# Four more idle matmuls on zeros between the second scores and the M1 of batch 0

**Chip, cores, metric.** One Trainium2 chip, one core. The metric is device time in microseconds (us) of one execution. Timed runs are compared with runs of the kernel before on the same chip in the same job. Ratios are the mean time of one kernel's fast runs over that of the other's fast runs of the same rounds, so they are not quite the ratio of the medians that are quoted beside them.

## The reference, cut to what matters

```python
p_packed = sm_attn(p, k, v)                  # 8 batches, 8 heads: 32 packed rows attend to 576 keys
x        = sm_attn(q, p_packed, p_packed)    # 576 queries attend to the 32 packed rows
h = x_as_tokens @ w_in                       # 4608 x 512 @ 512 x 2048
g = s * relu(h)**2 + b
out = g @ w_out                              # 2048 x 512
```

## The kernel before

The kernel is a fixed order of small steps ("words"). The words of batch 0 that matter here:

- `a` first attention (packed), which ends in `ppc` on VectorE; `c.0.0`, `c.0.1` second scores, the two halves of the columns, each followed by two exponentials on ScalarE;
- `w.0.0`, `w.0.1` the softmax's denominators: two matmuls, then `ld` (Ln) and `rcd` (Exp) on ScalarE, then `aT` on VectorE;
- `f.0.0`, `e.0.1`, `e.0.2`, `e.0.3` the four chunks of `pw` (packed rows times w_in), evicted by VectorE (f) or by ScalarE and VectorE (e); each needs its piece of w_in;
- `h.0.x` half groups of M1 (4 matmuls of 288 columns), evicted by `rlu` on ScalarE and squared on VectorE;
- `t`, the output matmuls `yps`; `z`, one idle matmul on zeros that is meant to keep TensorE's clock up.

```python
def big(dt=F32):                       # every TensorE result goes to such a tile: 2 x 512 float32 per partition
    w = NB if dt == F32 else 2 * NB
    rings["n"] += 1
    ps = rings["h"][rings["n"] % len(rings["h"])]      # two pools of 2 tiles: 4 tiles at this stage
    return ps.tile([P, 2, w], dt, tag="h", name="hps")

def idle(n):
    t = big()                          # an idle matmul takes a tile as well
    for x in range(n):
        mm(t[:, 0, :], zeros[:, 0:P], zeros[:], start=True, stop=True)

def weights_half(b, hf):               # the word w
    ...
    dps = big()
    for qd in range(NQ):
        mm(dps[:, qd, 0:HS], onesbd[:], e2[b][:, qd, cols], start=True, stop=True)
    ...
    act.activation(out=ld[:], in_=dps[:, :, 0:HS], func=AF.Ln)
    ...
    act.activation(out=rcd[:], in_=ld[:]..., func=AF.Exp, scale=-1.0)
    vec.tensor_tensor(out=aT[b][:, :, cols], in0=e2[b][:, :, cols], in1=rcd[:]..., op=ALU.mult)
```

The program pins the order of each engine's instructions (`keep_in_program_order`), and the trace of before has it: on ScalarE `ld` at 17.97, `rcd` at 18.67, the second pair at 19.26 and 19.93, then `pw` at 20.52 us. Which tile a word gets is decided when the program is built, and with it what it must wait for.

The softmax here doesn't subtract the row's maximum and nothing guards it: scores larger than these inputs give would overflow.

Of the kernel before, what the change touches and what calls it, by code (L numbers as in the profile page):

```python
# [13 lines left out]

ORDER = """
z kf kc kh.0.1 mask p.0.1 qh.0.0 qh.0.1 kT.0.1 kT.0.0 z z v.0 z win.0 win.1 pp2.0.1 pT.0 qT.0.1 z
s.0.0 s.0.1 qT.0.0 win.2 a.0.0 a.0.1 c.0.0 f.0.0 win.3 c.0.1 w.0.0 w.0.1 e.0.1 z h.0.2 h.0.0 e.0.2
wout.0 q.1 h.0.4 h.0.7 h.0.5 e.0.3 h.0.6 h.0.8 wout.1 h.0.1 h.0.11 h.0.13 k.1 h.0.3 four h.0.10 t.1
p.1.2 h.0.9 wout.2 t.2 h.0.15 qT.1.1 t.1 t.2 qT.1.0 b.0 t.0 h.0.12 t.0 v.1 b.1 pp2.1.2 t.1 kT.1.1
t.2 pT.1 wout.3 sb b.2 h.0.14 q.2 kT.1.0 t.1 t.0 t.0 b.3 s.1.0 s.1.1 t.0 t.1 k.2 t.1 p.2.8 a.1.0 b.4  # L20
a.1.1 q.3 b.5 b.6 b.7 c.1 t.1 t.0 t.1 e.1.0 w.1.0 t.0 t.0 w.1.1 v.3 t.2 qT.2.1 t.2 e.1.1 k.3 t.2 t.2
t.2 kT.2.0 pp2.2.8 m.1.0 three t.3 t.3 pT.2 kT.2.1 f.1.2 t.3 e.1.3 v.2 t.3 qT.2.0 t.3 m.1.8 m.1.1
m.1.6 m.1.14 m.1.13 m.1.3 t.3 m.1.5 m.1.10 qo.3 m.1.2 t.4 qD.3 s.2.0 m.1.7 m.1.9 m.1.11 t.4 s.2.1
m.1.4 m.1.12 kD.3 t.3 m.1.15 a.2.0 t.4 a.2.1 t.4 t.4 t.4 pT.3 k.4 c.2 t.4 t.4 t.3 E.2.0 w.2.0 t.6
t.6 t.5 w.2.1 t.6 t.5 t.5 vo.3 t.6 E.2.1 t.6 m.2.5 t.5 t.5 t.6 pT.4 t.6 s.3.0 s.3.1 t.6 m.2.1 t.5
m.2.3 a.3.0 m.2.13 t.5 m.2.10 a.3.1 t.7 q.4 t.7 t.7 c.3 t.5 qo.4 m.2.2 t.7 t.7 w.3.0 t.8 t.8 E.3.0
qD.4 t.8 t.8 kD.4 w.3.1 v.4 t.7 m.2.14 t.7 m.2.0 m.2.15 m.2.6 m.2.7 m.2.9 t.8 t.8 m.2.12 m.2.8
m.2.11 t.7 m.2.4 E.3.1 t.8 t.8 vo.4
"""

@with_exitstack
# [809 lines left out]
```

## Time and profile before

| | before |
|---|---|
| time, median of 3 (lowest to highest) | 255.1 us (254.94 to 255.21) |
| span of the profiled run | 252.8 us |
| busy: TensorE, VectorE, ScalarE | 95%, 57%, 57% |
| mean granted TensorE clock | 0.993 |
| first `yps` matmul of the output | 28.75 us |
| from there to the end | 224.1 us |

The mean clock is worth reading exactly: one window of 3.41 us at half clock (18.81 to 22.22 in the trace of before) lowers the mean over 252.8 us by 3.41 x 0.5 / 252.8 = 0.0067, so 0.993 is one halved window, about 0.987 two, 0.980 three (a halved piece at the very end takes up to 0.003 more: 1.3 us in the trace of before_again). The clock's first record begins at 11.98 us in the trace of before, and this is meant below where the clock "rose" at the start. Ahead of it matmuls of 512 columns start 0.43 us apart (9.43 to 9.86 in before), twice the 0.216 of the later ones at full clock.

The profiled execution of before took 254.62 us, 0.3 us less than the fastest of its timed runs: the trace that the prediction reads is of a quick execution.

The views that decide are shown in the prediction. One more, the order of time of TensorE before (start, length, engine, line, operation, count, idle before and its releaser):

```profile
16.98 1.46 PE L93 MATMUL hps<-e,onesbd 128*128 128x288 bf16 x4 [0.29 <-ACT e L104]
18.85 1.30 PE L93 MATMUL hps<-w_in_sb,ppc 64*32 64x512 bf16 x8 [0.42 <-DMA w_in_sb<-in_moe_w_in_dram]
20.48 2.00 PE L93 MATMUL hps<-aT,pw 128*128 128x288 bf16 x8
```

The first line is `w`: four matmuls that stream for 0.12 us each (288 columns; M1's of this width start 0.122 us apart at full clock), spread over 1.46 us because each waits for one exponential. "Busy" in the windows counts each matmul's modelled length (0.28 us for one of these) and overstates how much streams.

### The profile page before, as it was taken

The numbers are of one execution on the slowest core, as the hardware profiler recorded it, in microseconds if no ns is written. First come the engines' busy times: TensorE is split into PE (matmuls) and PEld (weight loads), VectorE is DVE, ScalarE is ACT, GpSimd is POOL, SyncE is SP. The second block draws the span as 40 slices with busy tenths as digits, with TensorE's granted clock in tenths as the row PEclk, the third lists the DMA queues.
The fourth block names the chain that finished last, engine by engine and source line by source line (L and its number), as shares of the span: only waits on it lengthen the run. The fifth ranks groups of instructions, "written<-read, shape, count | busy, mean of one in ns | idle before, by whom it ended". The sixth has DMA issues, their size and how long they took to land.

```text
span 252.8 us, 5625 instructions
## 1 busy us (share of the span) xinstructions
PE 240.3 (95%) x2326; PEld 137.5 (54%) x2326; DVE 145.3 (57%) x301; ACT 143.4 (57%) x220; POOL 32.8 (13%) x49
## 2 busy tenths in 40 slices
PE   0869999999999999999999999999999999999994
PEld 0644655457745656655565556645665545555442
DVE  3347742597657578666835676467734664453221
ACT  3178923738856698668664774478545854543000
POOL 8736242110021002100110021000000000000000
PEclk9997999999999999999999999999999999999999
DMA  7999999999679985996699679909412122111332
GB/s 147 190 201 205 204 203 205 195 239 212 117 124 185 183 148 89 220 181 137 134 174 194 124 148 163 225 22 178 99 38 52 34 60 70 41 41 44 83 83 83
DMA packets 54635, 34.61 MB, mean 137 GB/s; under 512 B 27345, under 2 KB 50129, under 8 KB 54609
## 3 DMA queue, kind: packets, MB, share of 16 engines
q0 software_dynamic: 24928, 18.32, 48.7%
q1 hardware_dynamic: 29584, 15.87, 27.5%
q8 instruction: 18, 0.29, 0.5%
q14 instruction: 9, 0.07, 0.1%
q10 hardware_dynamic: 96, 0.07, 0.1%
HBM read 37.23 MB, written 9.44 MB: 185 GB/s over the span
## 4 chain that ended last, share of the span: by engine, by line
PE 89%; DMA 4%; POOL 3%; ACT 1%; DVE 1%; issue 1%; POOLq 0%
PE yps L93 52%; PE hps L93 35%; DMA w_in_sb<-in_moe_w_in_dram 4%; PE hps L96 2%; POOL raw L104 2%; ACT rlu L104 1%; POOL w_in_sb L104 1%; DVE ysb L104 0%; ACT pw L104 0%; DVE pw L104 0%; POOL pn L104 0%; POOL identb L104 0%; POOLq L104 0%; POOLq L825 0%
## 5 line engine op out<-in xcount | busy, mean ns | idle before, releaser
L93 PE MATMUL yps<-w_out_sb,gT 128*128 128x512 bf16 (+2 forms) x592 | 144.6, 374 | 0.2 <-DVE ysb L104 0.2
L104 ACT ACTIVATE rlu<-hps 128x576 bf16<-128x576 f32 x128 | 80.6, 653 | 58.9 <-PE hps L93 52.9
L104 DVE TENSOR_TENSOR gT<-rlu 128x576 bf16<-128x576 bf16 x128 | 58.2, 456 | 57.6 <-ACT rlu L104 55.5
L93 PE MATMUL hps<-aT,pw 128*128 128x288 bf16 x512 | 80.7, 288 | 0.2 <-DVE pw L104 0.2
L93 PEld LDWEIGHTS <-gT 128*128 128x128 bf16 x592 | 53.5, 98 | 49.7 <-issue 7.2
L93 PEld LDWEIGHTS <-pw 128*128 128x128 bf16 x512 | 50.0, 99 | 31.8 <-issue 1.2
L104 DVE SCALAR_TENSOR_TENSOR ysb<-yps,svec,biasrep 128x512 f32<-128x512 f32 (+2 forms) x37 | 27.0, 732 | 16.5 <-PE yps L93 16.4
L104 DVE TENSOR_SCALAR pw<-hps,rd 128x1024 bf16<-128x1024 f32 (+1 forms) x22 | 22.5, 1036 | 1.0 <-PE hps L93 0.4
L104 ACT ACTIVATE pw<-hps,rd 128x1024 bf16<-128x1024 f32 (+1 forms) x18 | 17.5, 973 | 3.8 <-PE hps L93 3.7
L104 DVE TENSOR_TENSOR aT<-e,rcd 128x576 bf16<-128x576 bf16 x16 | 12.1, 757 | 9.9 <-ACT rcd L104 9.8
L104 POOL DMA_DIRECT2D raw<-in_k_dram x8 | 6.2, 779 | 85.2 <-DMA kT<-raw 62.5
L104 ACT ACTIVATE e<-hps,rs 128x576 bf16<-128x576 f32 (+1 forms) x18 | 11.3, 686 | 10.1 <-PE hps L93 10.1
L104 ACT ACTIVATE e<-hps 96x768 bf16<-96x768 f32 x16 | 12.5, 800 | 3.6 <-PE hps L93 3.5
L96 PE MATMUL hps<-identb,raw 96*64 96x96 bf16 (+1 forms) x216 | 9.5, 224 | 5.3 <-DMA raw<-in_k_dram 5.2
L96 PEld LDWEIGHTS <-raw 96*64 96x64 bf16 (+1 forms) x216 | 8.1, 117 | 8.2 <-DMA raw<-in_k_dram 6.0
L93 PE MATMUL hps<-w_in_sb,ppc 64*32 64x512 bf16 x256 | 11.6, 389 | 0.7 <-DMA w_in_sb<-in_moe_w_in_dram 0.4
L104 ACT ACTIVATE rcd<-ld 128x576 f32<-128x576 f32 x16 | 10.9, 683 | 0.5
L104 ACT ACTIVATE ld<-hps 128x576 f32<-128x576 f32 x16 | 10.3, 644 | 0.3 <-PE hps L93 0.2
L104 DVE COPY raw<-raw 96x1536 bf16<-96x1536 bf16 x20 | 10.4, 562 | 0.0
L93 PEld LDWEIGHTS <-ppc 64*32 64x32 bf16 x384 | 4.0, 89 | 9.4 <-issue 6.9
L93 PEld LDWEIGHTS <-raw 96*64 96x64 bf16 (+1 forms) x264 | 7.7, 106 | 2.5 <-issue 1.5
L104 POOL DMA_DIRECT2D raw<-in_q_dram x11 | 8.4, 777 | 3.8 <-PE hps L96 3.3
(45 smaller groups left out, 105.6 us busy)
## 6 DMA issues: line engine op xcount, KB each, us to landing
raw<-in_v_dram POOLq DMA_DIRECT2D x8, 576.0 KB, 11.2
out_dram<-ysb SPq DMA_DIRECT2D x23, 192.0 KB, 2.5
raw<-in_q_dram POOLq DMA_DIRECT2D x7, 576.0 KB, 11.8
raw<-in_k_dram POOLq DMA_DIRECT2D x7, 576.0 KB, 8.1
out_dram<-ysb SPq DMA_DIRECT2D x24, 128.0 KB, 2.4
w_in_sb<-in_moe_w_in_dram POOLq DMA_DIRECT2D x8, 256.0 KB, 10.8
w_out_sb<-in_moe_w_out_dram POOLq DMA_DIRECT2D x4, 512.0 KB, 14.8
out_dram<-ysb SPq DMA_DIRECT2D x23, 64.0 KB, 2.1
```

Source lines behind the costliest of these rows:

```text
L93: return tc.keep_in_program_order(nc.tensor.matmul(*a, **kw))
L96: return tc.keep_in_program_order(nc.tensor.transpose(*a, **kw))
L104: return lambda *a, **kw: tc.keep_in_program_order(f(*a, **kw))
```

## The change

Its intent: fill TensorE's waits between batch 0's second scores and its M1 with work on zeros, so that the clock isn't halved there.

```diff
-s.0.0 s.0.1 qT.0.0 win.2 a.0.0 a.0.1 c.0.0 f.0.0 win.3 c.0.1 w.0.0 w.0.1 e.0.1 z h.0.2 h.0.0 e.0.2
+s.0.0 s.0.1 qT.0.0 win.2 a.0.0 a.0.1 c.0.0 f.0.0 z win.3 c.0.1 z w.0.0 z w.0.1 e.0.1 z z h.0.2 h.0.0
+e.0.2 ...   (the rest of the order is the same, wrapped anew)
```

More of the change, by code (lines that the diff above doesn't have):

```diff
@@ L16 @@
 z kf kc kh.0.1 mask p.0.1 qh.0.0 qh.0.1 kT.0.1 kT.0.0 z z v.0 z win.0 win.1 pp2.0.1 pT.0 qT.0.1 z
-s.0.0 s.0.1 qT.0.0 win.2 a.0.0 a.0.1 c.0.0 f.0.0 win.3 c.0.1 w.0.0 w.0.1 e.0.1 z h.0.2 h.0.0 e.0.2
-wout.0 q.1 h.0.4 h.0.7 h.0.5 e.0.3 h.0.6 h.0.8 wout.1 h.0.1 h.0.11 h.0.13 k.1 h.0.3 four h.0.10 t.1
-p.1.2 h.0.9 wout.2 t.2 h.0.15 qT.1.1 t.1 t.2 qT.1.0 b.0 t.0 h.0.12 t.0 v.1 b.1 pp2.1.2 t.1 kT.1.1
-t.2 pT.1 wout.3 sb b.2 h.0.14 q.2 kT.1.0 t.1 t.0 t.0 b.3 s.1.0 s.1.1 t.0 t.1 k.2 t.1 p.2.8 a.1.0 b.4
-a.1.1 q.3 b.5 b.6 b.7 c.1 t.1 t.0 t.1 e.1.0 w.1.0 t.0 t.0 w.1.1 v.3 t.2 qT.2.1 t.2 e.1.1 k.3 t.2 t.2
-t.2 kT.2.0 pp2.2.8 m.1.0 three t.3 t.3 pT.2 kT.2.1 f.1.2 t.3 e.1.3 v.2 t.3 qT.2.0 t.3 m.1.8 m.1.1
-m.1.6 m.1.14 m.1.13 m.1.3 t.3 m.1.5 m.1.10 qo.3 m.1.2 t.4 qD.3 s.2.0 m.1.7 m.1.9 m.1.11 t.4 s.2.1
-m.1.4 m.1.12 kD.3 t.3 m.1.15 a.2.0 t.4 a.2.1 t.4 t.4 t.4 pT.3 k.4 c.2 t.4 t.4 t.3 E.2.0 w.2.0 t.6
-t.6 t.5 w.2.1 t.6 t.5 t.5 vo.3 t.6 E.2.1 t.6 m.2.5 t.5 t.5 t.6 pT.4 t.6 s.3.0 s.3.1 t.6 m.2.1 t.5
-m.2.3 a.3.0 m.2.13 t.5 m.2.10 a.3.1 t.7 q.4 t.7 t.7 c.3 t.5 qo.4 m.2.2 t.7 t.7 w.3.0 t.8 t.8 E.3.0
-qD.4 t.8 t.8 kD.4 w.3.1 v.4 t.7 m.2.14 t.7 m.2.0 m.2.15 m.2.6 m.2.7 m.2.9 t.8 t.8 m.2.12 m.2.8
-m.2.11 t.7 m.2.4 E.3.1 t.8 t.8 vo.4
+s.0.0 s.0.1 qT.0.0 win.2 a.0.0 a.0.1 c.0.0 f.0.0 z win.3 c.0.1 z w.0.0 z w.0.1 e.0.1 z z h.0.2 h.0.0
+e.0.2 wout.0 q.1 h.0.4 h.0.7 h.0.5 e.0.3 h.0.6 h.0.8 wout.1 h.0.1 h.0.11 h.0.13 k.1 h.0.3 four
+h.0.10 t.1 p.1.2 h.0.9 wout.2 t.2 h.0.15 qT.1.1 t.1 t.2 qT.1.0 b.0 t.0 h.0.12 t.0 v.1 b.1 pp2.1.2
+t.1 kT.1.1 t.2 pT.1 wout.3 sb b.2 h.0.14 q.2 kT.1.0 t.1 t.0 t.0 b.3 s.1.0 s.1.1 t.0 t.1 k.2 t.1
+p.2.8 a.1.0 b.4 a.1.1 q.3 b.5 b.6 b.7 c.1 t.1 t.0 t.1 e.1.0 w.1.0 t.0 t.0 w.1.1 v.3 t.2 qT.2.1 t.2
+e.1.1 k.3 t.2 t.2 t.2 kT.2.0 pp2.2.8 m.1.0 three t.3 t.3 pT.2 kT.2.1 f.1.2 t.3 e.1.3 v.2 t.3 qT.2.0
+t.3 m.1.8 m.1.1 m.1.6 m.1.14 m.1.13 m.1.3 t.3 m.1.5 m.1.10 qo.3 m.1.2 t.4 qD.3 s.2.0 m.1.7 m.1.9
+m.1.11 t.4 s.2.1 m.1.4 m.1.12 kD.3 t.3 m.1.15 a.2.0 t.4 a.2.1 t.4 t.4 t.4 pT.3 k.4 c.2 t.4 t.4 t.3
+E.2.0 w.2.0 t.6 t.6 t.5 w.2.1 t.6 t.5 t.5 vo.3 t.6 E.2.1 t.6 m.2.5 t.5 t.5 t.6 pT.4 t.6 s.3.0 s.3.1
+t.6 m.2.1 t.5 m.2.3 a.3.0 m.2.13 t.5 m.2.10 a.3.1 t.7 q.4 t.7 t.7 c.3 t.5 qo.4 m.2.2 t.7 t.7 w.3.0
+t.8 t.8 E.3.0 qD.4 t.8 t.8 kD.4 w.3.1 v.4 t.7 m.2.14 t.7 m.2.0 m.2.15 m.2.6 m.2.7 m.2.9 t.8 t.8
+m.2.12 m.2.8 m.2.11 t.7 m.2.4 E.3.1 t.8 t.8 vo.4
 """
```

## The prediction

Its sums come to 0.13 us faster (step 3), 0.21 us slower (step 4) and 255.1 us at even chances. In the paragraph that begins with "one window of 3.41 us", "them" are the instructions of ScalarE and VectorE, and the four tiles are the program's two pools of two. The 0.43 us of an idle matmul at half clock is twice 0.216, as M1's 0.240 is twice 0.122; it is also the spacing of the idle matmuls ahead of the clock's first record.

> **What bounds the kernel now.** I read the page first. Its second part cuts the span of 252.8 us into 40 slices of 6.3 us; these are the rows of TensorE, ScalarE and the granted TensorE clock, in tenths:
>
> ```profile
> PE   0869999999999999999999999999999999999994
> ACT  3178923738856698668664774478545854543000
> PEclk9997999999999999999999999999999999999999
> ```
>
> TensorE is full from slice 4 (19 us) on, so the kernel is TensorE-bound for nine tenths of its length and any time saved or lost before that shifts everything behind it. The one mark on the clock is the 7 in slice 4. So I cut the stretch around it into pieces of 3.41 us (columns: window, length, then busy us and count of TensorE, weight loads, VectorE, ScalarE, GpSimd; granted clock; DMA share; GB/s):
>
> ```profile
> 11.98:15.40 3.42, 2.93 (x105) 2.61 (x104) 0.92 (x2) 2.54 (x4) 0.94 (x2) 1.00 1.21 194
> 15.40:18.81 3.41, 2.04 (x36) 0.80 (x34) 1.94 (x5) 2.36 (x6) 1.21 (x2) 1.00 1.24 206
> 18.81:22.22 3.41, 3.27 (x17) 1.43 (x17) 2.18 (x3) 2.88 (x5) 2.25 (x3) 0.50 1.23 204
> 22.22:25.64 3.42, 3.23 (x36) 1.99 (x35) 2.69 (x6) 3.24 (x7) 2.31 (x3) 1.00 1.25 206
> ```
>
> The clock is halved for exactly one such window, 18.81 to 22.22, and the window before it is the one with the least TensorE work (2.04 us busy, against 2.93 and more). That is the target of the change: batch 0's softmax (c, w), where TensorE waits for ScalarE.
>
> Then the chain of work that ended last, for 14 to 36 us (start, length, what):
>
> ```profile
> 8.55 10.93 DMA w_in_sb<-in_moe_w_in_dram
> 19.53 2.97 PE hps L93 x16
> 22.52 0.65 ACT rlu L104
> ...
> 25.23 0.73 ACT pw L104
> 25.96 0.02 issue
> 25.98 0.76 DVE pw L104
> 26.75 0.04 issue
> 26.79 2.12 PE hps L93 x16
> ```
>
> Until 19.5 us the path is the load of w_in. Then come 3 us of TensorE at half clock; but from 22.5 to 26.8 the path is ScalarE and VectorE, not TensorE. That decides how much a faster TensorE is worth. The order of time on ScalarE there (start, length, what, count, idle before and its releaser):
>
> ```profile
> 16.42 1.68 ACT L104 ACTIVATE e<-hps,rs 128x288 bf16<-128x288 f32 x4 [1.77 <-PE hps L93]
> 17.97 0.67 ACT L104 ACTIVATE ld<-hps 128x576 f32<-128x576 f32 x1
> 20.52 0.67 ACT L104 ACTIVATE pw<-hps,rd 128x512 bf16<-128x512 f32 x1
> 21.69 0.65 ACT L104 ACTIVATE rlu<-hps 128x576 bf16<-128x576 f32 x1 [0.50 <-PE hps L93]
> 22.52 0.65 ACT L104 ACTIVATE rlu<-hps 128x576 bf16<-128x576 f32 x1 [0.18 <-PE hps L93]
> ```
>
> ScalarE is busy without a pause from 16.42 to 21.19, waits 0.50 and 0.18 us for the two slow M1 groups (h.0.2, h.0.0), and hardly pauses again before 28 us. Those 0.68 us are all that a warm clock can give back to ScalarE.
>
> [...]one window of 3.41 us at 0.50, and its M1 matmuls (288 columns) start 0.240 us apart, against 0.122 us at full clock. [...]the trace has them in program order everywhere I looked, so a late ld delays all that follows it on ScalarE. [...]there are four tiles at this stage, and every idle matmul takes one: it isn't free even where TensorE waits.
>
> **The change, part by part.** The built programs show what it does: ScalarE, VectorE, GpSimd and SyncE have exactly the same instructions and waits; TensorE gets four weight loads and four 128x512 matmuls; and because each takes a PSUM tile, eleven or so waits in this stretch change. From the first M1 groups after the fourth chunk of pw onwards everything is the same again.
>
> 1. The four matmuls themselves. A 512-column one costs 0.216 us of TensorE at full clock (the spacing of the later yps matmuls: 28.746 to 28.962), 0.43 at half. One comes before c.0.1 (16.38 to 16.60): c.0.1 then ends at 16.91 instead of 16.69, but ScalarE takes it only at 17.21; free. One before w.0.0, one between w.0.0 and w.0.1: TensorE waits there anyway. The fourth is behind e.0.1, which waits for w_in until 19.49; it ends near 20.2 (warm) and h.0.2 can't start before aT is ready; free when warm.
>
> 2. A new wait, the cost of the change. w.0.0 used to start with one exponential done each (matmuls at 16.98 and 17.37), so ScalarE ran ld directly behind the four exponentials, at 17.97. Now the extra tiles push w.0.0 onto the tile that c.0.1 has just used, so it waits for the fourth exponential, which ends at 18.10. Then 0.05 us of semaphore (17.317 to 17.368 in the trace), 0.12 to the second matmul, 0.28 its length, 0.04 to ScalarE: ld starts at 18.59, 0.62 us later. ScalarE's queue moves with it: both ld/rcd pairs, aT (VectorE 20.01 instead of 19.39), pw of e.0.1 (ScalarE 21.13, VectorE ends 22.68 instead of 22.06).
>
> 3. The gain, if the clock stays full. h.0.2 waits for aT, so it starts at about 20.88 (before 20.48), and needs 0.49 instead of 0.96 us: ends 21.53. ScalarE's rlu then follows pw without a pause at 21.70 (before 21.69), the next at 22.23 (22.52): of the 0.68 us of pauses, 0.62 were spent on the late ld. e.0.2 no longer waits for an rlu, but its w_in lands at 22.01, so it starts at 22.05; h.0.4 needs VectorE's pw: 22.73 (22.76 before). pw of e.0.2 on ScalarE 22.76 (23.07), rlu of h.0.4 at 23.42 (23.64): 0.2 us ahead. Then e.0.3: its last piece of w_in lands at 24.61 in the trace, and it started at 24.59 and 24.65 before. It can't move, so its pw starts at 25.10 at best instead of 25.23. Sum: 0.13 us faster.
>
> 4. If the clock still drops. e.0.1 at 19.53, two idle matmuls of 0.43, h.0.2 at 20.94, its rlu at 22.15 (before 21.69), h.0.0's at 22.75 (22.52), pw of e.0.3 at 25.44 (25.23). Sum: 0.21 us slower.
>
> Which of the two? Columns streamed in the window from 15.40: about 1.1 us before (0.15 of packed, 0.12 + 0.12 of c, 0.22 of f, 4 x 0.12 of w), 32%; now plus 3 x 0.216, 51%. The window ahead of it, by the same rough count about 2.2 us or 65%, did not drop the clock. 51% lies in the middle of the bracket; I call it even.
>
> **Rivals.** (a) The full prize of the throttle: 3.41 us at half clock is 1.7 us of lost array time, so 253.4 us. For it speaks that TensorE bounds the rest; against it the chain, which from 22.5 to 26.8 runs over ScalarE and VectorE, and w_in's landings at 22.01 and 24.61. (b) The late ld goes through undiminished, 0.62 us: 255.7 us. That needs ScalarE's pauses of 0.68 us not to close; only if the clock drops and the window falls otherwise. (c) The matmuls cost their own time on the path: 4 x 0.216 = 0.86 us, 256.0 us. Against it: each stands in a wait. (d) [...]other executions drop the clock elsewhere than this profile. The three timed runs lie within 0.27 us of each other, so this is small.
>
> **Range and chances.** Even chances of -0.13 and +0.21 give 255.1 us. Run-to-run spread (254.94 to 255.21) and an error of some tenths in the waits make the range 254.5 to 255.7. Two per cent is 5.1 us, three times the whole loss to the clock; I give 0.98 to "within 2%", 0.01 to each side.
>
> **What would show it.** ld of batch 0 near 18.6 instead of 17.97, and aT near 20.0: step 2. The granted clock in the window from about 18.8: 1.00 is step 3, 0.50 step 4; h.0.2's matmuls 0.122 or 0.240 apart. ScalarE's pause before the first rlu gone: step 3. The e.0.3 matmuls still near 24.6 and the first M1 group after pw of e.0.3 at 26.6 to 27.0 instead of 26.79: the sum. From there to the end the same length, 226.1 us. I am wrong if that group moves by over half a microsecond, or if the rest of the span changes length.

## The result

The changed kernel took 254.6 us (median of 4 runs, 254.37 to 254.96) against 255.12 us (4 runs, 254.94 to 255.21): ratio 0.9982, 95% interval 0.9964 to 0.9999. The profiled run was the slowest of its four, at a mean clock of 1.000. It is inside the predicted range. But the two traces do not show where half a microsecond went, and the profiled span, 253.2 us, is longer than before's 252.8.

The page's rows of TensorE and the granted clock after, 40 slices of the span in tenths:

```profile
PE   0877999999999999999999999999999999999994
PEclk9999999999999999999999999999999999999999
```

The 7 of the clock is gone. The windows of 3.41 us, on this run's own boundaries (window, length, busy us and count of TensorE, weight loads, VectorE, ScalarE, GpSimd; granted clock; DMA share; GB/s):

```profile
12.31:15.72 3.41, 2.67 (x104) 2.41 (x102) 0.92 (x2) 2.25 (x4) 0.63 (x2) 1.00 1.20 192
15.72:19.14 3.42, 2.40 (x40) 1.12 (x36) 1.95 (x5) 1.79 (x4) 2.29 (x3) 1.00 1.24 205
19.14:22.55 3.41, 2.50 (x29) 1.13 (x27) 1.51 (x3) 3.34 (x6) 1.96 (x3) 1.00 1.24 205
```

The stretch that was at 0.50 is at 1.00. TensorE in order of time after; the third line is `w.0.0`, which now waits for the fourth exponential:

```profile
17.05 0.39 PE L93 MATMUL hps<-zeros 128*128 128x512 bf16 x1
17.37 0.32 PE L93 MATMUL hps<-qT,ppc 64*32 64x288 bf16 x8
18.70 0.40 PE L93 MATMUL hps<-e,onesbd 128*128 128x288 bf16 x2 [0.59 <-ACT e L104]
```

ScalarE in order of time after:

```profile
16.79 1.86 ACT L104 ACTIVATE e<-hps,rs 128x288 bf16<-128x288 f32 x4 [1.96 <-PE hps L93]
19.15 0.65 ACT L104 ACTIVATE ld<-hps 128x576 f32<-128x576 f32 x1 [0.49 <-PE hps L93]
21.67 0.67 ACT L104 ACTIVATE pw<-hps,rd 128x512 bf16<-128x512 f32 x1
22.24 1.18 ACT L104 ACTIVATE rlu<-hps 128x576 bf16<-128x576 f32 x2
25.57 0.70 ACT L104 ACTIVATE pw<-hps,rd 128x512 bf16<-128x512 f32 x1
```

The two `rlu` now follow `pw` without the pauses of 0.50 and 0.18 us, and a new pause of 0.49 us stands before `ld`: from the first exponential to `ld` it is 2.36 us, against 1.55 before. The end of this stretch in the chain of work (start, length, what):

```profile
25.57 0.71 ACT pw L104
26.30 0.76 DVE pw L104
27.11 2.12 PE hps L93 x16
```

The same three links as before, 0.32 us later. Ahead of them the chain has changed: before, it was the load of w_in until 19.49, then TensorE at half clock; now it is ScalarE's queue, from the late `ld` at 19.15 to this `pw` with no wait for another engine. All of the 0.32 us was there before the changed stretch: the load of `v.0` landed at 14.46 us in this trace and at 14.08 in the one before, and `ppc` on VectorE, which starts batch 0's second attention, was at 16.06 instead of 15.69. Counted from `ppc`, the first `yps` matmul comes after 13.00 us (before: 13.06), and 224.1 us remain in both. In these two traces the change is worth 0.06 us after `ppc`: the late `ld` took what the clock gave. So the half microsecond between the medians had to come from executions that were not profiled.

### The profile page after: what moved, and what is told of

Same layout as the page of the kernel before. It is cut to its first block, busy times and chain, and to the rows that moved or that the text cites. A ratio compares the mean times of both kernels' runs of the same rounds, so it can differ in the third digit from the quotient of the medians.

```text
span 253.2 us, 5632 instructions
## 1 busy us (share of the span) xinstructions
PE 239.6 (95%) x2330; PEld 137.3 (54%) x2330; DVE 145.1 (57%) x301; ACT 143.5 (57%) x220; POOL 32.8 (13%) x49
## 4 chain that ended last, share of the span: by engine, by line
PE 89%; DMA 3%; ACT 3%; POOL 2%; DVE 1%; issue 1%; POOLq 0%; ACTq 0%
PE yps L93 52%; PE hps L93 35%; DMA raw<-in_v_dram 3%; PE hps L96 2%; POOL raw L104 1%; ACT rlu L104 1%; ACT pw L104 1%; ACT rcd L104 1%; ACT ld L104 0%; DVE ysb L104 0%; ACT e L104 0%; DVE pw L104 0%; POOL pn L104 0%; POOL identb L104 0%; DVE ppc L104 0%
## 5 line engine op out<-in xcount | busy, mean ns | idle before, releaser
L93 PE MATMUL hps<-aT,pw 128*128 128x288 bf16 x512 | 79.8, 286 | 1.6 <-DVE aT L104 0.9
L104 DVE TENSOR_TENSOR aT<-e,rcd 128x576 bf16<-128x576 bf16 x16 | 12.1, 758 | 10.5 <-ACT rcd L104 10.4
L104 ACT ACTIVATE e<-hps,rs 128x576 bf16<-128x576 f32 (+1 forms) x18 | 11.4, 685 | 10.4 <-PE hps L93 10.3
L93 PE MATMUL hps<-w_in_sb,ppc 64*32 64x512 bf16 x256 | 11.0, 382 | 0.0
L104 DVE COPY raw<-raw 96x1536 bf16<-96x1536 bf16 x20 | 10.4, 561 | 0.0
L93 PE MATMUL hps<-e,raw 96*64 96x32 bf16 (+1 forms) x264 | 8.5, 188 | 0.7 <-DMA raw<-in_v_dram 0.7
```

Source lines behind the costliest of these rows:

```text
L93: return tc.keep_in_program_order(nc.tensor.matmul(*a, **kw))
L104: return lambda *a, **kw: tc.keep_in_program_order(f(*a, **kw))
```

## The experiments

Theory: the new waits make `ld` late by about 0.6 us, the full clock closes ScalarE's pauses, and the time depends on which windows are halved. Rivals: the clock alone gives TensorE its lost time back; the tiles' new places are the gain; the loads of `v.0` and w_in make all differences. Each kernel gave a correct result. After each label: median, median of before in the same job, ratio with its 95% interval.

**before_again**: no edit.

> The kernel before against itself, to show how far two medians of five rounds lie apart when nothing differs. All theories: ratio 1.000, medians within 0.2 us; clock 0.993 in nearly all runs (one halved window of 3.41 us at about 19 us). If some of its runs show 1.000, the phase of the window decides and not the kernel alone.

254.93 us against 255.15 us; 0.9989 (0.9965 to 1.0012). Nothing differs, and the result is 0.1% with an interval of 0.5%. The clocks were 0.993 in 2 of 6 runs and 0.984 to 0.987 in 4: two halved windows are the common case, and the trace of before had shown the rarer one. The trace of this run has two (columns as above):

```profile
16.35:19.76 3.41, 3.25 (x37) 0.91 (x38) 1.76 (x5) 2.70 (x6) 1.96 (x3) 0.50 1.24 206
19.76:23.18 3.42, 2.89 (x17) 1.13 (x17) 2.61 (x4) 2.91 (x6) 1.85 (x3) 0.50 1.23 204
```

From `ppc` to the first `yps` it is 12.98 us there, no more than the 13.06 with one: the first of the two lies where TensorE mostly waits for ScalarE (in the trace of before the four matmuls of `w` stream for 4 x 0.122 of 1.46 us). So a second halved window need not cost anything there; where the windows lie counts as well as how many they are. Part of what this run lost lies ahead of `ppc`: the clock rose at 12.94 instead of 11.98, and `ppc` followed the landing of `v.0` by 1.86 us instead of 1.61.

**after_again**: the changed kernel, no edit.

> The changed kernel once more, with more rounds. My theory (late ld +0.62 us, ScalarE's pauses closed, e.0.3 held by the load of w_in): 0.1 to 0.3 us faster than before. Rival (the clock alone: 3.41 us at half speed given back to TensorE): 0.8 us or more faster, and the runs whose mean clock is 1.000 faster than those at 0.993. Second rival (noise of the load of v.0 and w_in): no difference.

255.96 us against 255.15 us; 1.0009 (0.9978 to 1.0040). The ratio fits the second rival's "no difference" and rules out the first rival's 0.8 us; the 0.1 to 0.3 us of my theory lie inside the interval, but its point is not met. None of the three foresaw what the runs show, that they fall into two groups by the clock: 254.13 (clock 0.993) and 254.42 (1.000), and 255.93 to 256.28 (0.985 to 0.987). The profiled run was of the late group. Two of its windows (columns as above):

```profile
17.78:21.19 3.41, 2.72 (x15) 0.80 (x14) 1.23 (x2) 2.62 (x6) 2.14 (x3) 0.50 1.24 203
21.19:24.61 3.42, 3.42 (x20) 1.59 (x20) 2.42 (x5) 2.92 (x5) 1.81 (x4) 0.50 1.24 206
```

Here the window boundaries lay at 14.37 and 17.78, the clock fell at 17.78 and stayed low for two windows. ScalarE in that run:

```profile
19.14 0.65 ACT L104 ACTIVATE ld<-hps 128x576 f32<-128x576 f32 x1 [0.72 <-PE hps L93]
22.53 0.65 ACT L104 ACTIVATE rlu<-hps 128x576 bf16<-128x576 f32 x1 [0.20 <-PE hps L93]
23.49 0.65 ACT L104 ACTIVATE rlu<-hps 128x576 bf16<-128x576 f32 x1 [0.31 <-PE hps L93]
24.95 1.74 ACT L104 ACTIVATE rlu<-hps 128x576 bf16<-128x576 f32 x3 [0.17 <-PE hps L93]
```

The late `ld` is paid and the pauses stay as well: 14.47 us from `ppc` to the first `yps`.

**no_tile**: the same four matmuls in the same places, without a tile of their own.

```diff
+    def warm(t):
+        mm(t, zeros[:, 0:P], zeros[:], start=True, stop=True)
 ...second_scores_half:
         t = big()
+        if hf == 1:
+            warm(t[:, 0, :])
 ...weights_half:
         dps = big()
+        warm(dps[:, 0, :])
 ...order (zz is idle(2): two matmuls in one tile):
-w.0.0 w.0.1 e.0.1 z h.0.2
+w.0.0 w.0.1 e.0.1 zz h.0.2
```

The first real matmul into the tile has its start flag set.

> The same four idle matmuls, at the same places, but written into the PSUM tile that the next real group takes anyway, so no tile is taken and no wait is new. All theories: ld stays near 17.97 us (after the landing of v.0 is allowed for), clock 1.000 as often as in the changed kernel. My theory (the load of w_in holds e.0.3 at about 24.65 whatever happens before): no better than the changed kernel, 0.1 to 0.3 us faster than before. Rival (the late ld costs 0.62 us on the path): 0.6 us faster than the changed kernel.

254.98 us against 255.15 us; 0.9981 (0.9958 to 1.0003). Two runs at 1.000 took 254.06 and 254.2 us, four at 0.991 to 0.993 took 254.93 to 255.14. ScalarE of the profiled run (clock 1.000):

```profile
16.60 1.80 ACT L104 ACTIVATE e<-hps,rs 128x288 bf16<-128x288 f32 x4 [1.78 <-PE hps L93]
18.29 0.65 ACT L104 ACTIVATE ld<-hps 128x576 f32<-128x576 f32 x1
21.39 1.18 ACT L104 ACTIVATE rlu<-hps 128x576 bf16<-128x576 f32 x2
```

`ld` comes 1.69 us after the first exponential, with no pause, and there is none before `rlu` either. From `ppc` to the first `yps` it is 12.49 us, against 13.00 in the changed kernel at the same clock: some 0.5 us for the late `ld`, of which 0.06 are a difference in the load of w_in (below). Nor do four idle matmuls cost their own 0.86 us, as rival (c) of the prediction had it. The load of w_in does show as a floor once the rest is quicker (TensorE in order of time):

```profile
24.08 0.73 PE L93 MATMUL hps<-w_in_sb,ppc 64*32 64x512 bf16 x8
```

`e.0.3` began at 24.08 and spread over 0.73 instead of 0.41 us, because its last piece of w_in landed at 24.36.

**tile_only**: the changed kernel's tiles and waits, with one column in each added matmul.

```diff
-    def idle(n):
+    def idle(n, w=NB):
         t = big()
         for x in range(n):
-            mm(t[:, 0, :], zeros[:, 0:P], zeros[:], start=True, stop=True)
+            mm(t[:, 0, 0:w], zeros[:, 0:P], zeros[:, 0:w], start=True, stop=True)
 ...order (o is idle(1, 1)):
-f.0.0 z win.3 c.0.1 z w.0.0 z w.0.1 e.0.1 z z h.0.2
+f.0.0 o win.3 c.0.1 o w.0.0 o w.0.1 e.0.1 z o h.0.2
```

> The same four tiles taken and the same waits, but each new idle matmul has one column instead of 512, so the array does nothing more. My theory (the waits cost, the clock gives): clock 0.993 in nearly all runs, ld late as in the changed kernel, 0.2 us slower than before. Rival (the gain comes from the other places of the tiles, which free h.0.0 and e.0.2 from waiting for rlu): as fast as the changed kernel with the clock at 0.993.

256.03 us against 255.15 us; 1.0018 (0.9983 to 1.0053). Clock never 1.000. ScalarE of its trace:

```profile
16.87 1.68 ACT L104 ACTIVATE e<-hps,rs 128x288 bf16<-128x288 f32 x4 [1.78 <-PE hps L93]
19.04 0.65 ACT L104 ACTIVATE ld<-hps 128x576 f32<-128x576 f32 x1 [0.49 <-PE hps L93]
```

`ld` is late (2.17 us after the first exponential, 0.62 more than before, the figure of step 2) with no added work on the array. So the tiles alone cause it. The medians lie 0.9 us apart, the means 0.5; the interval excludes neither zero nor the 0.2 us that I expected. Four of six runs had two halved windows or more and took 255.97 to 256.97 us. The two with one took 254.22 and 254.39, like before's with one (254.34 on average). So the new places of the tiles are no gain; but the late `ld` cost nothing in these two runs either. Where the halved window fell in those two no trace shows.

**no_tile_more**: as no_tile, with eleven idle matmuls (`warm(t, n)` repeats n times).

```diff
 ...second_scores_half:
-        if hf == 1:
-            warm(t[:, 0, :])
+        warm(t[:, 0, :], 1)
 ...weights_half:
-        warm(dps[:, 0, :])
+        warm(dps[:, 0, :], 2)
 ...packed_w1 (the words e and f):
         t = big()
+        if b == 0 and ch == 1:
+            warm(t[:, 0, :], 4)
```

> Eleven idle matmuls in place of four, all in tiles that the next real group takes anyway (1 before each half of c, 2 before each half of w, 4 before e.0.1, 1 more before h.0.2), so that no window of 3.41 us stays under the share that the first runs bracket (clock kept at 0.45 of the window streaming, dropped at 0.41). My theory (the state of the clock decides the time, and with a full clock the load of w_in is the floor): clock 1.000 in all runs, median near 254.2 us, the spread under 0.5 us, 0.3 to 0.4% faster than before. Rival (runs at 1.000 are only by chance the fast ones, and eleven matmuls cost time on the path): median over 255 us.

254.35 us against 255.39 us; 0.9966 (0.9934 to 0.9997). The clock was 0.998 or 1.000 in five runs, 0.993 in one (255.56 us). So the expectation "in all runs" failed by one and the spread was wider, 253.99 to 255.56 us; one run at 1.000 took 255.18, so the clock does not explain all of it. From `ppc` to the first `yps`: 12.25 us.

**no_tile_more_again**: the same, another job.

> The version with eleven idle matmuls in tiles taken anyway, once more. My theory: at least five of six runs at a clock of 0.990 or more, median 254.2 to 254.6 us. Rival (its first job was luck): median within 0.1% of before, several runs near 255.5 us.

254.25 us against 255.22 us; 0.9973 (0.9947 to 0.9999), five of six at 0.998 or more. The gain stands in both jobs. From `ppc` to the first `yps` this trace has 12.69 us, 0.44 more than the other of the same kernel at the same clock; all of it is a later `c.0.1`, held by the load of w_in (below).

**after_more**: the changed kernel, with more idle matmuls in the tiles it takes.

```diff
-f.0.0 z win.3 c.0.1 z w.0.0 z w.0.1 e.0.1 z z h.0.2
+f.0.0 z win.3 c.0.1 zz w.0.0 zz w.0.1 e.0.1 zz z h.0.2      (here zz is idle(3))
```

> The changed kernel with its idle matmuls tripled in three of the four places, same tiles, same new waits: the late ld stays, but the clock should be full in every run. My theory (with a full clock the late ld is hidden behind the load of w_in and costs 0.2 us at most): clock 1.000, median 254.3 to 254.6 us, the late runs near 256 us gone. Rival (the late ld costs its 0.6 to 0.9 us in every state, as the late runs suggest): median near 255 us, 0.8 us over the version that takes no tiles.

255.47 us against 255.39 us; 1.0000 (0.9967 to 1.0033). Two runs at 1.000 took 254.56 and 254.57 us, as expected for that state, but four still had one halved window and took 255.35 to 256.04 us. So filling the waits after `c.0.1` wasn't enough in those four; where their windows lay no trace shows. From `ppc` to the first `yps` at full clock: 13.01 us, the same as the changed kernel's 13.00, and 0.76 and 0.32 us over the two traces of no_tile_more.

**more_e3_later**: no_tile_more with `e.0.3` one M1 group later.

```diff
-h.0.5 e.0.3 h.0.6 h.0.8
+h.0.5 h.0.6 e.0.3 h.0.8
```

> The version with eleven idle matmuls, and e.0.3 (the group that waits for the last piece of w_in) one M1 group later in TensorE's order. Theory of the floor as w_in's landing: first yps matmul 0.1 to 0.4 us earlier than in the version without this move, time 254.0 us or less. Rival (ScalarE, busy without a pause from 16 to 28 us, is the floor): no change, or later by up to 0.3 us because pw of e.0.3 comes later.

254.34 us against 255.39 us; 0.9955 (0.9926 to 0.9983), all six runs at 0.998 or 1.000. The first `yps` came 12.43 us after `ppc`, between the two traces without the move (12.25 and 12.69): no sign here that the landing of w_in's last piece is what holds that version, though so few traces are little.

**more_e3_again**: the same, another job.

> The version with eleven idle matmuls in tiles taken anyway and e.0.3 one M1 group later, once more, since one job's median moves with the states of the clock. My theory (no run with two halved windows at 19 us): at least five of six runs at a clock of 0.990 or more, median 254.3 us, 0.2 to 0.5% faster than before. Rival (its first job was luck): median within 0.1% of before.

254.85 us against 255.22 us; 0.9984 (0.9950 to 1.0017). Three runs at 253.84 to 254.19 us, three with a halved window at 255.51 to 255.77. The move of `e.0.3` shows no gain over the version without it, and the expected 254.3 us were missed. The trace is of a run with a halved window, 16.78 to 20.20, and has 13.62 us from `ppc` to the first `yps`. The window before it (13.37 to 16.78) lies almost wholly ahead of the second scores (`ppc` came at 16.29), where this version and no_tile_more add nothing.

**warm_all** and **warm_all_e3**: eleven more idle matmuls at the very start and two before `a.0.0`, without and with the move of `e.0.3`.

```diff
-z kf kc kh.0.1 mask
+z0 kf kc kh.0.1 mask             (z0 is idle(12))
 ...packed:
         pp = pps[b]
+        if b == 0 and qd == 0:
+            warm(pp[:, 0, :], 2)
```

> The eleven-matmul version with 11 more at the very start (5 us at half clock while the first k is on its way) and 2 in the wait for v.0, all in tiles taken anyway. My theory (the phase of the window makes the spread, at the start as well as at 19 us): the clock rises before 10.5 us in the trace, ppc follows the landing of v.0 by 1.6 us and not by up to 2.8, the spread shrinks under 0.6 us, median 253.9 to 254.2. Rival (the spread is the loads): spread and median as in the eleven-matmul version.

> The same with e.0.3 one M1 group later. If the load of w_in is the floor: 0.1 to 0.3 us faster than without the move. If ScalarE is: no change within 0.2 us.

255.49 and 254.65 us against 254.78 us; 1.0026 (0.9995 to 1.0057) and 0.9998 (0.9978 to 1.0018). The clock did rise at 7.0 and 5.5 us instead of 10.4 to 13.9, and `ppc` followed `v.0` by 1.60 and 1.59 us, as expected (2.76 in no_tile_more). The spread did not shrink: 254.22 to 256.86 us in the first, with halved windows in four of six runs. Where the clock fell in those runs no trace shows. Whether the move of `e.0.3` helps here stays open: the two medians are 0.84 us apart, but so are the states of their runs. The trace of warm_all_e3 needs 13.89 us from `ppc` to the first `yps` at full clock and with no tile added: TensorE waited 1.19 us in `f.0.0` for a piece of w_in that landed at 17.12.

**after_third**: the changed kernel once more.

> The changed kernel again, for the share of its runs in each state of the clock. From the ten runs so far: mean clock 1.000 or 0.993 at 254.1 to 255.0 us, 0.980 to 0.988 near 256 us; the median of the job follows from how many fall in each, so anywhere from 0.5 us faster to 0.8 us slower than before. My theory (late ld and full clock cancel): from VectorE's ppc to the first yps matmul 13.0 us at full clock, 14.4 with two halved windows, as in the traces so far (13.00 and 14.48). Rival (the change is a gain in itself): three quarters of the runs or more under 254.9.

255.28 us against 254.78 us; 1.0022 (0.9994 to 1.0050). Three runs at 254.18 to 254.86 us, three at 255.71 to 256.17 (clock 0.987). Half the runs are late, so the rival falls. Its trace has one halved window, 17.24 to 20.66, and 13.21 us from `ppc` to the first `yps`, between the full clock's 13.00 and the 14.47 with two.

### All timed runs by the state of their clock

Full is a mean clock of 0.997 or more, one a single halved window (0.990 to 0.993), two is two or three (0.980 to 0.987); mean time and, in brackets, the number of runs. The first job's runs of before have no clock on record and are left out.

| kernel | full | one | two or three | all, mean |
|---|---|---|---|---|
| before | none | 254.34 (14) | 255.36 (36) | 255.08 (50) |
| changed | 254.69 (4) | 254.40 (5) | 255.99 (7) | 255.17 (16) |
| tile_only | none | 254.31 (2) | 256.39 (4) | 255.70 (6) |
| no_tile | 254.13 (2) | 255.04 (4) | none | 254.74 (6) |
| no_tile_more, both jobs | 254.33 (10) | 255.39 (2) | none | 254.50 (12) |

The changed kernel has fewer runs with two halved windows (7 of 16 against 36 of 50, which so few runs do not put beyond chance), and takes 0.6 us more in these on average; where one window or none is halved it is no faster than before with one. On average the two cancel: 255.17 against 255.08 us. The same count need not mean the same windows, though: no_tile with one halved window takes 0.7 us more than before with one. In the first job none of its four runs happened to have two halved windows, while before's lay at 255.1 us like its runs with two; that would explain the 0.18%, but isn't shown, since the clocks of those runs of before aren't on record. The same kernel stood at 0.9982, 1.0009 and 1.0022 in its three jobs. All of it happens ahead of the first `yps`: from there to the end it is 224.0 to 224.5 us in every one of the 14 traces.

The loads, the third rival, are not out; they are part of the spread. `v.0` landed between 13.52 and 14.97 us in the 14 traces, and `ppc` waits for it. Behind `ppc`, `c.0.1` stands after `f.0.0` in TensorE's order, and so waits for that word's piece of w_in (and, where there is one, for the idle matmul between them): its first exponential came 0.38 or 0.39 us after the one before where the piece landed early, and 0.50 to 1.88 us after it where the piece landed over half a microsecond after `ppc` at full clock. Taking this delay out of the time from `ppc` to the first `yps`, the eight traces at full clock fall into two groups: 12.25 to 12.51 us in the six without added tiles, 12.82 in both with them (after, after_more). So the late `ld` costs 0.3 to 0.6 us at full clock, and the loads do not explain it. How much of the spread between executions that were not profiled is clock and how much is loads, no run here separates.

What comes before a halved window? I added up, in all 14 traces, how long TensorE streamed columns in each window (columns times 0.42 ns, from 0.216 us for 512, without overlaps). At full clock, windows of 0.29 to 0.42 were followed by half clock and windows of 0.45 and more were not. Upwards the traces give no clean cut: at half clock, windows of 0.72 were followed by half clock in one trace and by full in another, and in no_tile_more one of 0.90 (7.03 to 10.44) by half. In the trace of before the window ahead of the drop (15.40 to 18.81) has no stretch without streaming over 0.6 us; the sum is 0.29. Six of the 14 traces have a drop in the stretch studied: in three the clock rose again after one window, of which streaming filled 0.72 to 0.88, in three it stayed low through a window filled to 0.60, 0.72 and 0.73, and rose after the next. This is a reading of 14 traces by one measure, not a rule shown by an experiment of its own.

## Why the prediction was right, and where it wasn't

The range held, the class held, and the point was 0.5 us above the first job's median and within 0.1 us of the mean of all 16 runs. That the class held says little: two per cent is three times the whole loss to the clock. That the range held was partly luck: seven of the 16 runs, and the median of after_again (255.96), lie above its upper end of 255.7. Of its own signs, most came as written: the late `ld`, the full clock, M1 matmuls 0.122 us apart, no pause before the first `rlu`, 226.0 us from the group after `pw` of `e.0.3` to the end (226.1 before). That group stood at 27.11, 0.1 past its bracket, with `ppc` 0.37 later. By its steps:

1. The cost of the idle matmuls themselves: right for three of them. The one before `c.0.1` was called free and was not quite. In the profiled run `f.0.0` waited for w_in until 16.72 (16.17 before, without a wait), so the idle matmul stood at 17.05, `c.0.1` at 17.37 and its first exponential at 17.76, where ScalarE had had it 0.4 us after the one before. It came 0.57 us after it: 0.19 us lost.
2. The late `ld`: right in its mechanism and its size. Predicted 0.62 us; tile_only shows 0.62, the changed kernel 0.81, of which 0.19 is the point above.
3. The gain at full clock: the sum was right (predicted -0.13 us, measured 13.00 instead of 13.06 us from `ppc` to the first `yps`), but partly by luck, since one reason failed: "It can't move, so its pw starts at 25.10 at best instead of 25.23". In the changed kernel's trace the last piece landed at 24.69 and `e.0.3` began at 24.84, so it did not wait; what held its `pw` was ScalarE's queue behind the late `ld`. no_tile, without the late `ld`, is 0.5 us shorter at the same clock. The landing varies between traces (23.95 to 24.78 us), and in no_tile it shows as a floor, lower than I put it.
4. "If the clock still drops": mis-sized. I took for granted that a drop lasts one window, because before's trace showed one. With one halved window the loss was 0.06 us by the mean times and 0.15 by the traces (13.21 against 13.06), near the 0.21 predicted; with two it was 0.6 us against before in the same state. That the clock can stay low through a second window was not in the sum. This is rival (b), the late `ld` undiminished, which the prediction kept for the case that "the window falls otherwise": seven of 16 runs lie at its 255.7 us or above, and in the one that was traced the pauses stayed, as it says.

Rival (d), that other executions drop the clock elsewhere, I set aside on the ground that three timed runs lay within 0.27 us. That was the weakest step: 50 runs of the same kernel go from 253.92 to 256.45 us, and the state of the clock largely sorts them; in the traces the halved stretch began at 18.81 us (before), 16.35 (before_again), 17.78 (after_again) and 17.24 (after_third). It did not break the prediction because the two errors that follow from it happen to cancel, which is luck. The estimate that 51% of a window lies "in the middle of the bracket" rested on a wrong reading: adding up the columns of all matmuls gives 0.67 for the earlier window, near the 65%, because matmuls that overlap count twice (the eight of `c.0.0`, 288 columns each, all start between 16.035 and 16.058 us), while the 32% counts them once. By the one measure above the two windows of before are 0.50 and 0.29, the changed kernel's are 0.45 and 0.46, and in the 14 traces the edge lies between 0.42 and 0.45.

Rival (a), the full prize of 1.7 us, is out for the changed kernel: its runs at full clock are no faster than before's with one halved window. Part of the prize is there without the tiles: no_tile_more beats before by 0.3% (0.9966 and 0.9973, each interval just under 1). Against the changed kernel it was not run in one job; the means over different jobs are 254.50 and 255.17 us. It is the version to keep, though not a sure one: with `e.0.3` moved, the same idle matmuls left a halved window in three of six runs of one job.

## What to carry to other kernels

Work that is put into a wait still takes buffers, and the waits that the buffers bring can cost as much as the work gives (here the late `ld`, 0.3 to 0.6 us at full clock); here the idle matmuls belong in the tile that the next group takes anyway. When the state of the clock decides, one trace shows one state of it (that of before one halved window, which 14 of 50 runs had): look at the clock of every timed run before believing half a per cent, and run the kernel against itself first. What a faster TensorE gained here ended at ScalarE's queue (0.06 us after `ppc`), so ask from the chain what lies behind the engine that you make faster.
